# Attention and soft-MoE on one core: 128-row input tiles for later batches, a PSUM bank for each half of the first output tile, 12 one-column products, and a new instruction order

## The chip, the cores and the metric

The kernel runs on one core of one Trainium2 chip. The core has five engines with a queue each: PE (matrix products), ACT, DVE and POOL (elementwise work), and SP; 16 DMA engines carry all transfers. The metric is the device time of one launch in microseconds, the median of three runs. Before the change it is 151.72 us (151.67 to 151.9).

## The reference

Attention over four batches, eight heads, 768 positions and a head size of 64; heads with `is_retrieval` have the full causal mask, the others see four sink positions and a window of 64. Its output, 3072 rows of 512, goes through a soft mixture of eight experts with four slots each.

```python
scores = np.where(mask, scale * q @ k.T, -1e9)
a = softmax(scores); x = (a @ v)                     # [4, 8, 768, 64] -> [3072, 512]
logits = x @ phi                                     # 32 slots
slot_input = softmax(logits, axis=0).T @ x           # [32, 512]
for e in range(8):
    slot_out[e] = np.maximum(slot_input[e] @ w1[e], 0) @ w2[e]
out = softmax(logits, axis=1) @ slot_out
```

Inputs are float32: q, k and v of 6.3 MB each, and 16 expert matrices of 2 MB each (w1 and w2). The output is 6.3 MB.

## The kernel before

Every load but two small ones is issued from POOL's queue and cast to bfloat16 on its way into SBUF: 12 loads of q, k, v (one for each batch and tensor, 96 rows of 8 KB) and 16 of weights (128 rows of 8 KB), 26 MB as written. They go into 12 buffers ("slot") and, for the last four weights, into memory that attention has done with (Lw12 to Lw15).

The kernel is a list of named operations. Each declares its engine, what it depends on and which buffers it takes and gives back; the text ORDER at the head of the file is the order in which all of them are emitted, so it fixes the order on each engine. A suffix /A, /D or /P puts an operation on ACT, DVE or POOL. The names:

- Lq, Lk, Lv, Lw (line 241): loads. Tx b.c (line 389): 16 transposes on PE that bring a quarter of x of batch b into head-major form; Ex b.c (lines 234 and 236): the copy out of PSUM. V2 and VB: the same for v by key block. VF (line 456): v times a head mask.
- QK.p.g (line 408), EX.p.g (line 476), MK.p.g (line 420): scores, exponential (ACT) and mask (DVE) of head pair p (16 of them, p = 4b + n) and group g; PV.p.i (line 524) the products with v, NM (lines 535 and 537) the division, XT and XE the transposed result. QX and EXX: a last block of scores for all four pairs of a batch.
- LG, EL, TE, EG, DS, SA: logits, exponentials, dispatch sums into the slots. After the last batch: SI, SIE (the slots' inputs), H and HR (w1 and relu, line 689 and 699), TH and HE (transposes), W2.e (line 744: w2 of expert e, 16 products in four column groups, W2.7 in two halves, the first for columns 0 to 255), SO.0 and SO.1 (lines 759 and 761: each half of the slots' output, scaled), EE and RW (the combine weights and their sums).
- OMf m (line 769) and OEf m (lines 774 and 776): output tile m of 24, a product of 128 x 512 and its scaled copy out of PSUM; tile 0 is done in two halves, 0L and 0R. STf gi.r (line 804, SP's queue): the ten stores, from 256 KB to 1 MB.
- Z0 to Z67 (line 332): products of zeros, placed between the others. Z5 is eight of them between W2.6 and W2.7. "warm" is 18 of them at the start.

W2.5, W2.6 and W2.7 need the loads Lw13, Lw14 and Lw15, which are issued once the memory that they overwrite is free: Lw14 after DS.2, Lw15 after the last scores of batch 3.

Of the kernel before, what the change touches and what calls it, by code (L numbers as in the profile page):

```python
# [20 lines left out]
Lri zero warm Lq0 tables ident Lk0 keypos Tq0.3 flags Tq0.1 Z0 hm0 Eq0.1/A Tq0.2 Eq0.3/D Eq0.2/A Tq0.0 slottab  # L21
Z62 Tk0.3 Eq0.0/D Ek0.3/D ones Tk0.0 Lv0 Z60 Tk0.2 Ek0.0/D Tk0.1 Z61 Ek0.1/D Ek0.2/A QK.0.1 Tv0.1 hm3 Lw0 Lq1
Ev0.1/D EX.0.1 QK.0.0 Tv0.0 EX.0.0 QK.0.3 Ev0.0/D Lk1 EX.0.3 Tv0.2 MK.0.1 Tv0.3 Z66 hm1 Ev0.2/D QK.0.2 Ev0.3/A
Z64 MK.0.3 MK.0.0 V2.0 EX.0.2 QX.0 VB.0/A Z63 V2.3 hm2 QK.0.4 V2.1 VF.0/D VB.3/D MK.0.2 EXX.0 PV.0.0 QK.1.1
EX.0.4 V2.2 Lphi0 PV.0.1 PV.0.2 VB.2/D QK.1.0 PV.0.3 Lv1 EX.1.1 VB.1/D Lw1 Tq1.1 MK.1.1 QK.1.3 EX.1.0 MK.0.4
Tq1.0 MK.1.0 EX.1.3 QK.1.4 EX.1.4 Lw2 Eq1.0/D PV.0.4 PV.0.5 Eq1.1/D QK.2.2 Tq1.3 EX.2.2 NM.0 VF.3/P QK.1.2
VF.1/P Eq1.3/D VF.2/P EX.1.2 Tk1.3 MK.1.3 PV.1.0 QK.2.1 Tq1.2 Ek1.3/D PV.1.1 QK.2.3 MK.1.2 EX.2.1 Tk1.1 PV.1.2
MK.1.4 QK.2.0 EX.2.3 Eq1.2/D PV.1.3 PV.1.4 Ek1.1/D EX.2.0 MK.2.1 MK.2.3 Lq2 QK.2.4 MK.2.0 PV.1.5 EX.2.4 QK.3.4
Tk1.0 Tk1.2 NM.1 QK.3.3 MK.2.2 Lphi1 EX.3.4 EX.3.3 PV.2.0 PV.2.1 QK.3.0 EX.3.0 PV.2.2 Ek1.2/D PV.2.3 Lk2
Ek1.0/D XT.1 QK.3.1 MK.2.4 MK.3.3 EX.3.1 PV.2.4 PV.2.5 XE.1/D QK.3.2 XT.0 NM.2 XE.0/D EX.3.2 Tv1.1 Z67 MK.3.0  # L30
MK.3.1 QK.4.4 MK.3.2 Ev1.1/A Lv2 EX.4.4 QK.4.2 Tv1.2 Ev1.2/D MK.3.4 Tv1.0 EX.4.2 PV.3.0 PV.3.1 QK.4.0 Lw3
Tv1.3 PV.3.2 Ev1.0/D QK.4.1 Ev1.3/D PV.3.3 EX.4.0 PV.3.4 V2.4 MK.4.0 Lw4 EX.4.1 QK.4.3 VB.4/D PV.3.5 V2.6
QK.5.0 XT.2 Lw5 EX.4.3 Z65 NM.3 VB.6/A XT.3 XE.2/D EX.5.0 MK.4.1 MK.4.3 XE.3/A QK.5.3 Lq3 Tq2.1 QK.5.1 VF.4/P
MK.5.0 PV.4.0 Eq2.1/D Tq2.0 PV.4.1 EX.5.3 Tq2.2 QX.1 MK.4.2 phi PV.4.2 EX.5.1 EXX.1 PV.4.3 Eq2.2/A MK.5.1
MK.4.4 LG.0 Eq2.0/D QK.5.4 MK.5.3 Tk2.2 Ek2.2/D EL.0 V2.5 EX.5.4 PV.4.4 VB.5/D QK.5.2 TE.0 PV.4.5 Lk3 EX.5.2
MK.5.4 EG.0/D VF.5/P QK.6.0 Tk2.0 NM.4 Ek2.0/D QK.6.1 EX.6.0 MK.5.2 DS.0 QK.6.4 VF.6/P PV.5.0 EX.6.1 PV.5.1
V2.7 SA.0 PV.5.2 QK.6.2 EX.6.4 MK.6.0 PV.5.3 Tv2.1 QK.6.3 PV.5.4 PV.5.5 EX.6.2 MK.6.1 VB.7/D Ev2.1/D XT.4
QK.7.1 Lv3 EX.6.3 MK.6.4 XE.4/A Tk2.1 MK.6.2 QK.7.4 NM.5 MK.6.3 EX.7.1 Tk2.3 PV.6.0 Ek2.1/D PV.6.1 Ek2.3/D
PV.6.2 EX.7.4 QK.7.2 Tq2.3 PV.6.3 QK.7.0 Lw6 EX.7.2 MK.7.1 Eq2.3/D PV.6.4 MK.7.2 PV.6.5 EX.7.0 QK.7.3 Tv2.0
QK.8.2 EX.7.3 NM.6 Ev2.0/D EX.8.2 VF.7/P Tv2.2 Lw7 MK.7.0 QK.8.0 Tv2.3 PV.7.0 PV.7.1 QK.8.1 EX.8.0 Ev2.2/D  # L40
EX.8.1 XT.6 PV.7.2 QX.2 EXX.2 MK.7.3 Ev2.3/D V2.11 XE.6/D MK.7.4 PV.7.3 MK.8.1 VB.11/D QK.8.3 MK.8.2 V2.8
PV.7.4 QK.8.4 PV.7.5 V2.10 EX.8.3 VB.8/D MK.8.0 NM.7 EX.8.4 XT.5 QK.9.1 VF.8/P VB.10/A QK.9.3 EX.9.1 PV.8.0
PV.8.1 PV.8.2 XT.7 XE.5/D MK.8.3 MK.8.4 V2.9 QK.9.2 XE.7/D PV.8.3 PV.8.4 EX.9.3 VB.9/D QK.9.0 PV.8.5 Tq3.0
MK.9.3 VF.10/P MK.9.1 Tq3.2 EX.9.2 QK.10.2 NM.8 EX.9.0 VF.9/P Eq3.2/D LG.1 Tq3.1 EX.10.2 EL.1 Lw8 QK.9.4
Eq3.0/D MK.9.0 Tk3.2 Eq3.1/D MK.9.2 QK.10.0 PV.9.0 EX.9.4 EX.10.0 TE.1 MK.10.2 EG.1/D PV.9.1 PV.9.2 QK.10.1
Tk3.0 MK.9.4 PV.9.3 Ek3.2/D QK.10.3 Ek3.0/D EX.10.1 PV.9.4 PV.9.5 QK.10.4 EX.10.3 MK.10.0 Tk3.3 NM.9 EX.10.4
QK.11.2 Ek3.3/D DS.1 EX.11.2 PV.10.0 QK.11.0 MK.10.1 Tk3.1 PV.10.1 SA.1 EX.11.0 QK.11.1 Tq3.3 VF.11/P Ek3.1/D
# [8 lines left out]
TE.2 XT.12 QK.15.1 PV.14.0 EX.14.4 MK.14.2 PV.14.1 MK.14.3 QK.15.0 EX.15.1 PV.14.2 PV.14.3 QK.15.2 EX.15.0
MK.14.4 PV.14.4 PV.14.5 EX.15.2 XE.12/D MK.15.1 QK.15.3 EG.2/D VF.15/P XT.13 EX.15.3 QK.15.4 EX.15.4 MK.15.0
NM.14 XE.13/D DS.2 PV.15.0 XT.14 MK.15.2 MK.15.3 MK.15.4 PV.15.1 XE.14/A PV.15.2 PV.15.3 SA.2 PV.15.4 PV.15.5
NM.15 LGa.3 LTa XT.15 XE.15/D Z1 LTb ET LGb.3 Z2 Lw14 Lw15 DS.3 Z3 SA.3 SI EL.3 SIE EE.0/A Z4 H.0.1 H.0.0
HR.0.1/A H.1.1 HR.0.0/A EE.1/D TH.0 EE.2/A EE.3/D HE.0/D HR.1.1/D H.1.0 RW HR.1.0/A W2.0 W2.1 TH.1 RWR W2.2  # L60
W2.3 HE.1/D W2.4 RC W2.5 W2.6 Z5 W2.7.0 SO.0/A W2.7.1 OMf0L SO.1/D OEf0L OMf0R OMf1 OMf2 OMf3 OEf0R OMf4 OMf5
OMf6 OEf1/A OEf2/D OMf7 OMf8 STf0.0 OEf3/A OMf9 OEf7/A STf0.1 OEf8/A OEf4/D OMf10 OEf5/D OMf11 STf0.2 OMf12
OEf6/D OMf13 OEf12/A OMf14 OEf9/A OMf15 OMf16 OEf11/A STf1.0 STf1.2 OEf10/A OMf17 OMf18 OEf17/D STf2.0 OMf19
OEf13/D OEf14/D OMf20 OEf15/D OMf21 OMf22 OEf21/A OEf19/D OMf23 STf2.2 OEf16/A OEf18/D OEf22/D STf3.0 OEf23/D
STf4.0 OEf20/D STf5.0
# [76 lines left out]
def kernel(  # L142
# [40 lines left out]
    phf = sb.tile([P, 4, NS], F32, name="phf")  # L183
# [10 lines left out]
    ri = sb.tile([P, 2 * H], I32, name="ri")  # L194
# [3 lines left out]
    edist = sb.tile([P, 640], BF16, name="edist")  # L198
# [6 lines left out]

    xflat = xT.rearrange("p a c -> p (a c)")
# [51 lines left out]
    wland = [None] * NW  # L258
# [6 lines left out]
    def load_w(i, deps=()):  # L265
# [4 lines left out]
        wland[i] = load(f"Lw{i}", "POOL", 2 << 20, None if i in late_mem else wbuf[i],  # L270
                        lambda: w_view(i), src, deps=deps)
# [37 lines left out]
    def emit_slot_tables(o):  # L309
# [24 lines left out]
    tlast = [pl.op("warm", "PE", deps=[o_zero], acq=[warm], rel=[warm], emit=lambda o: emit_zero(warm, 18))]  # L334
# [16 lines left out]
    o_phi = pl.op("phi", "DVE", deps=o_ph, emit=lambda o: nc.vector.tensor_copy(  # L351
# [10 lines left out]
    for x in "qkv":  # L362
        load_qkv(x, 2)
    for i in (3, 4, 5):
        load_w(i)
    for x in "qkv":
        load_qkv(x, 3)
# [476 lines left out]
```

## Time and profile before

| | before |
|---|---|
| median of three runs | 151.72 us |
| the profiled execution | 151.93 us |
| its span, first to last instruction | 150.1 us |
| busy: PE, DVE, ACT, POOL | 131.4, 113.3, 107.7, 33.5 us |
| mean granted TensorE clock | 0.977 |
| moved by DMA | 32.91 MB |
| PE instructions: products, weight loads | 2313, 2313 |

The span is 1.8 us shorter than the execution: what lies around the program's own instructions. Busy time is an average over stages; in the page's slices each digit is a busy share in tenths. A matmul's end is modelled, so a busy PE isn't PE at its peak. "issue" in the chain is time in which the engine waited for nothing that the profile shows. Queue 0 carries the loads, queue 1 the stores, queue 8 packets of instructions.

### The profile page before, as it was taken

What the parts mean: (1) busy time and instruction counts of PE and PEld (TensorE: products, weight loads), DVE (VectorE), ACT (ScalarE), POOL (GpSimd) and SP (SyncE); (2) the same over time, 40 slices, a digit from 0 to 9 for tenths busy, and PEclk for the clock granted to TensorE, in tenths of its full rate; (3) what the DMA queues carried; (4) which work ended last, traced back from release to release, by engine and by line L of the source; (5) the groups of instructions that cost most, each with busy time, mean ns of one, the idle gap of its engine ahead of it and who ended that gap; (6) DMA issues with size and microseconds to landing.
All of it is one profiled execution on the core that took longest, in us unless ns stands there. A gap on an engine that the chain in (4) does not pass through costs nothing.

```text
span 150.1 us, 5228 instructions
## 1 busy us (share of the span) xinstructions
PE 131.4 (87%) x2313; PEld 82.6 (55%) x2313; DVE 113.3 (76%) x257; ACT 107.7 (72%) x124; POOL 33.5 (22%) x51
## 2 busy tenths in 40 slices
PE   6999799999999999999989999999899999386100
PEld 2355456677666656767856576666564376132000
DVE  3955598999879599999997999999994542187800
ACT  3023699999899999999969999999964650286100
POOL 6910004760113070502450200604120000000000
PEclk9999999999999999999999999999999999999955
DMA  3999999999999999999999999999999998059995
GB/s 36 197 216 229 214 203 215 214 224 223 200 213 215 217 218 223 218 199 219 212 215 218 227 212 216 207 223 212 223 212 212 216 216 168 11 188 410 430 419 229
DMA packets 6950, 32.91 MB, mean 219 GB/s; under 512 B 1296, under 2 KB 1296, under 8 KB 4496
## 3 DMA queue, kind: packets, MB, share of 16 engines
q0 software_dynamic: 4800, 26.22, 85.2%
q1 hardware_dynamic: 2128, 6.37, 10.8%
q8 instruction: 18, 0.29, 0.7%
q14 instruction: 4, 0.03, 0.1%
HBM read 52.50 MB, written 6.29 MB: 392 GB/s over the span
## 4 chain that ended last, share of the span: by engine, by line
PE 49%; DMA 21%; DVE 15%; ACT 3%; issue 3%; POOL 2%; DVEq 0%; POOLq 0%; ACTq 0%
PE ps L408 13%; DMA qk<-in_moe_w_dram 13%; PE ps L524 12%; PE ps L389 9%; DMA slot<-in_v_dram 8%; DVE pt L420 5%; DVE slot L776 4%; PE ps L440 3%; PE ps L549 3%; DVE xv L537 3%; ACT pt L476 2%; PE ps L332 2%; PE ps L769 2%; PE ps L563 2%; DVE qk L236 2%
## 5 line engine op out<-in xcount | busy, mean ns | idle before, releaser
L476 ACT ACTIVATE pt<-ps 128x1024 bf16<-128x1024 f32 x80 | 77.6, 1026 | 4.9 <-PE ps L408 3.5
L420 DVE TENSOR_TENSOR pt<-pt,msk 128x512 bf16<-128x512 bf16 (+1 forms) x80 | 37.8, 503 | 1.2 <-ACT pt L476 1.2
L408 PE MATMUL ps<-qk 64*128 64x512 bf16 (+3 forms) x256 | 32.5, 309 | 0.0
L524 PEld LDWEIGHTS <-pt 128*128 128x128 bf16 x640 | 24.7, 97 | 9.1 <-issue 6.4
L524 PE MATMUL ps<-vx,pt 128*128 128x65 bf16 x352 | 27.9, 193 | 0.9 <-DVE xv L537 0.7
L389 PE MATMUL ps<-ident,slot 96*64 96x96 bf16 x768 | 24.1, 208 | 1.6 <-DMA slot<-in_v_dram 0.9
L456 POOL TENSOR_TENSOR vf<-vx,fm 128x528 bf16<-128x528 bf16 x14 | 15.5, 1114 | 44.3 <-DVE vx L236 42.5
L389 PEld LDWEIGHTS <-slot 96*64 96x64 bf16 x768 | 18.9, 109 | 10.6 <-issue 7.7
L524 PE MATMUL ps<-vf,pt 128*128 128x65 bf16 x288 | 22.7, 195 | 0.0
L332 PE MATMUL ps<-zero 128*128 128x512 bf16 x66 | 19.6, 431 | 1.2 <-DVE zero L323 1.2
L236 DVE COPY qk<-ps 128x768 bf16<-128x768 bf16 x28 | 14.9, 550 | 4.6 <-PE ps L389 4.4
L537 DVE TENSOR_TENSOR xv<-ps,rs 128x768 bf16<-128x768 f32 x16 | 15.3, 958 | 0.6
L408 PEld LDWEIGHTS <-qk 64*128 64x128 bf16 x256 | 9.2, 94 | 7.2 <-issue 1.6
L241 POOL DMA_DIRECT2D slot<-in_moe_w_dram x12 | 6.8, 565 | 22.7 <-PE ps L389 16.3
L236 DVE COPY xT<-ps 128x768 bf16<-128x768 bf16 (+1 forms) x15 | 8.6, 570 | 4.2 <-PE ps L710 3.2
L332 PEld LDWEIGHTS <-zero 128*128 128x128 bf16 x66 | 6.1, 108 | 9.3 <-issue 4.8
L234 ACT COPY qk<-ps 128x768 bf16<-128x768 bf16 x4 | 3.2, 797 | 10.7 <-PE ps L389 10.7
L776 DVE TENSOR_SCALAR slot<-ps,rrow 128x512 f32<-128x512 f32 (+1 forms) x14 | 9.2, 723 | 2.2 <-PE ps L769 2.2
L236 DVE COPY xv<-ps 128x768 bf16<-128x768 bf16 x14 | 7.7, 552 | 2.0 <-PE ps L389 2.0
L769 PE MATMUL ps<-msk,xv 128*128 128x512 bf16 (+1 forms) x25 | 6.5, 369 | 2.5 <-ACT slot L774 1.3
L774 ACT ACTIVATE slot<-ps,rrow 128x512 f32<-128x512 f32 (+1 forms) x11 | 6.6, 671 | 2.1 <-PE ps L769 2.1
L549 PE MATMUL ps<-ident,xv 128*128 128x128 bf16 x96 | 8.1, 220 | 0.0
(96 smaller groups left out, 129.0 us busy)
## 6 DMA issues: line engine op xcount, KB each, us to landing
slot<-in_moe_w_dram POOLq DMA_DIRECT2D x12, 1024.0 KB, 25.4
slot<-in_q_dram POOLq DMA_DIRECT2D x4, 768.0 KB, 18.4
slot<-in_k_dram POOLq DMA_DIRECT2D x4, 768.0 KB, 21.5
slot<-in_v_dram POOLq DMA_DIRECT2D x4, 768.0 KB, 23.7
out_dram<-slot SPq DMA_DIRECT2D x3, 1024.0 KB, 6.3
out_dram<-slot SPq DMA_DIRECT2D x5, 512.0 KB, 4.3
qk<-in_moe_w_dram POOLq DMA_DIRECT2D x2, 1024.0 KB, 18.8
vx<-in_moe_w_dram POOLq DMA_DIRECT2D x1, 1024.0 KB, 21.4
```

The costliest lines, as they stand in the source:

```text
L236: nc.vector.tensor_copy(dst, src)
L332: nc.tensor.matmul(scb[buf.slot][:, 0, :], zero[:, 0:128], zero, start=True, stop=True)
L389: nc.tensor.transpose(t[64 * i:64 * (i + 1), :, s, :], rv[:, i, 8 * c + s, :], ident[0:96, 0:96])
L408: nc.tensor.matmul(scb[sc.slot][:, i, c:c + 128 * nb], kk, qq.rearrange("p b c -> p (b c)"), start=True, stop=True)
L420: e.tensor_tensor(pT[:, :, 0:w], pT[:, :, 0:w], mh[:, :, c:c + w], op=ALU.mult)
L456: e.tensor_tensor(vfs[VFb[p].slot], vv, mm, op=ALU.mult)
L476: nc.scalar.activation(pTs[PTb[b, n].slot][:, :, 512 * g:512 * (g + 1)], scb[sc.slot], ACT.Exp, scale=scale)
L524: nc.tensor.matmul(pvb[:, h, 65 * i:65 * (i + 1)], lt, rhs, start=(j == 0), stop=(j == i))
L537: nc.vector.tensor_tensor(xo, pvw[:, :, :, 0:64], r.rearrange("p i (j o) -> p i j o", o=1).to_broadcast([P, 2, 6, 64]), op=ALU.mult)
L549: nc.tensor.transpose(t[:, 128 * i:128 * (i + 1)], xv[:, i, 128 * n:128 * (n + 1)], ident)
L769: nc.tensor.matmul(bank()[:, c0:c1], out_lhs(gi, r), slot_out[:, c0:c1], start=True, stop=True)
L776: nc.vector.tensor_scalar(d, bank()[:, c0:c1], sc_, None, op0=ALU.mult)
```

## The change

Six things change together.

1. **Tiles of 128 rows.** q, k, v of batch 0 stay as they were. Those of batches 1 to 3, 9 x 96 = 864 rows, are laid end to end into seven buffers of 128 rows (the last has 96). A tensor that crosses a buffer's edge is loaded in two pieces: q3, k1, v1 and v2. A group of 16 transposes now covers 128 rows, 28 groups instead of 36, and each tensor in it has a copy of its own out of PSUM (52 copies instead of 36). QK and V2 wait only for the pieces that hold their rows (`evs`).
2. **A bank for each half of tile 0.** OMf0L and OMf0R are two units with a PSUM bank each; they shared one.
3. **One-column products.** 12 products of 128 x 1 follow the 18 of "warm".
4. **Z5 is dropped**; the eight zero products between W2.6 and W2.7 go.
5. Setup: the slot tables are split, the larger part on POOL; phi's copy goes to ACT; `edist`, `phf` and `ri` live in the memory of eT.
6. **ORDER** is a new list, with other engines for some copies: SO.0 on DVE and SO.1 on ACT, all four HR on ACT.

```diff
+    tiles = [[(x, 0, 0, 0, 96)] for x in "qkv"]
+    row = 0
+    for b_, x_ in [(b_, x_) for b_ in range(1, B) for x_ in "qkv"]:
+        r0 = 0
+        while r0 < 96:
+            if row % 128 == 0:
+                tiles.append([])
+            n_ = min(96 - r0, 128 - row % 128)
+            tiles[-1].append((x_, b_, row % 128, r0, n_))
+            row, r0 = row + n_, r0 + n_
+    tbufs = [Buf("S8") for _ in tiles]
...
+    def emit_warm(o):
+        emit_zero(warm, 18)
+        for _ in range(12):
+            nc.tensor.matmul(scb[warm.slot][:, 0, 0:1], zero[:, 0:128], zero[:, 0:1], start=True, stop=True)
...
-                        nc.tensor.transpose(t[64 * i:64 * (i + 1), :, s, :], rv[:, i, 8 * c + s, :],
-                                            ident[0:96, 0:96])
+                        nc.tensor.transpose(t[64 * i:64 * (i + 1), :, s, :], rv[:, i, 8 * c + s, :],
+                                            ident[0:rows, 0:rows])
...
+    def evs(x, b, n=None):
+
+        return [o for r0, o in ev[x, b] if n is None or r0 < 24 * n + 24]
...
-            if e == NE - 1 and not z5:
-                z5 = [fill("Z5", 8, w2o[-1:] + [o_rwm])]
...
+    if not NLEFT:
+        units[:1] = [[(0, 0, 256)], [(0, 256, 512)]]
...
-H.1.0 RW HR.1.0/A W2.0 W2.1 TH.1 RWR W2.2
-W2.3 HE.1/D W2.4 RC W2.5 W2.6 Z5 W2.7.0 SO.0/A W2.7.1 OMf0L SO.1/D OEf0L OMf0R OMf1 OMf2 OMf3 OEf0R OMf4 OMf5
+W2.0 W2.1 W2.2 W2.3
+HE.1/D W2.4 Lw15 W2.5 W2.6 W2.7.0 W2.7.1 SO.1/A SO.0/D OMf0L OMf0R OMf1 OMf2 OEf0R OMf3 OEf0L OMf4 OEf1/A OMf5
```

What the change moves on the engines shows at three places. The first is PE's queue at the end of W2.7 and the first output tiles, before: line 744 is W2.7, line 769 OMf0L, OMf0R and OMf1.

```order
L744 LDWEIGHTS xT
L744 MATMUL ps<-qk_76,xT 32x256
L769 LDWEIGHTS xv
L769 MATMUL ps<-msk,xv 128x256 [waits Activation_49]
L769 LDWEIGHTS xv [waits DVE_49]
L769 MATMUL ps<-msk,xv 128x256 [waits Activation_49]
L769 LDWEIGHTS xv
L769 MATMUL ps<-msk,xv 128x512
```

The same place after the change (line 790 is W2.7, line 815 the output tiles):

```order
L790 LDWEIGHTS xT
L790 MATMUL ps<-qk_76,xT 32x256
L815 LDWEIGHTS xv
L815 MATMUL ps<-msk,xv 128x256 [waits DVE_49]
L815 LDWEIGHTS xv
L815 MATMUL ps<-msk,xv 128x256 [waits Activation_49]
L815 LDWEIGHTS xv
L815 MATMUL ps<-msk,xv 128x512
```

Before, OMf0R waits twice: for DVE (SO.1) and for ACT, which has to read OMf0L out of the bank. After, it waits once, for SO.1, now on ACT. These rows stand at 4575 to 4582 of PE's 4628 before, and at 4327 to 4334 of 4380 after.

The second place is PE's queue at the products that wait for the last two loads. Before, between W2.6 (from xv, the load Lw14) and W2.7 (from qk, Lw15), rows 4527 to 4532:

```order
L744 LDWEIGHTS xT
L744 MATMUL ps<-xv,xT 32x256
L332 LDWEIGHTS zero
L332 MATMUL ps<-zero 128x512
L332 LDWEIGHTS zero
L332 MATMUL ps<-zero 128x512
```

After, rows 4295 to 4300:

```order
L790 LDWEIGHTS xT
L790 MATMUL ps<-xv,xT 32x256
L790 LDWEIGHTS xT
L790 MATMUL ps<-qk_76,xT 32x256 [waits DMASW7_49]
L790 LDWEIGHTS xT
L790 MATMUL ps<-qk_76,xT 32x256
```

W2.6 is now followed at once by the product that waits for Lw15. W2.5 stands in rows 4233 to 4264 and W2.6 in rows 4265 to 4296.

The third place is POOL's queue, the loads behind those of batch 0. Before:

```order
L241 DMA slot_66<-in_moe_w_dram 128x4096
L241 DMA slot_67<-in_q_dram 96x2x2048
L241 DMA slot_68<-in_k_dram 96x2x2048
L241 DMA slot_69<-in_v_dram 96x2x2048
L241 DMA slot_70<-in_moe_w_dram 128x4096
```

After:

```order
L243 DMA slot_67<-in_q_dram 96x2x2048
L243 DMA slot_67<-in_k_dram 32x2x2048
L243 DMA slot_68<-in_k_dram 64x2x2048
L243 DMA slot_68<-in_v_dram 64x2x2048
L243 DMA slot_69<-in_v_dram 32x2x2048 [waits DMASW0_49]
L243 DMA slot_70<-in_moe_w_dram 128x4096 [waits DMASW1_49]
```

k1 and v1 are two loads each and share buffers with their neighbours. A load waits for the eighth one ahead of it (DMASW), which holds before and after.

More of the change, by code (lines that the diff above doesn't have):

```diff
@@ L20 @@
 ORDER = """
[L21 to L25, printed above, removed]
@@ L31 @@
[L31 to L35, printed above, removed]
@@ L56 @@
[L56 to L60, printed above, removed]
@@ L61 @@
-W2.3 HE.1/D W2.4 RC W2.5 W2.6 Z5 W2.7.0 SO.0/A W2.7.1 OMf0L SO.1/D OEf0L OMf0R OMf1 OMf2 OMf3 OEf0R OMf4 OMf5
[L62 to L65, printed above, removed]
+zero Lri warm Lq0 tables ident keypos Tq0.3 Tq0.2 Eq0.3/A Eq0.2/A Z0 Tq0.0 flags hm0 Lk0 hm3 Tq0.1 Lv0
@@ L66 @@
+OEf20/A STf5.0
 """
@@ L374, with transposes @@
     setup = [o_fl, o_id]
-    def transposes(x, b):
-        raw = raws[x, b]
-        tb = {"q": QTb, "k": KTb, "v": VTb}[x][b]
-        dst = {"q": lambda: qTs[QTb[b].slot], "k": lambda: kTs[KTb[b].slot], "v": lambda: vT}[x]
-        ev[x, b] = []
+    def transposes(g):
+        parts, raw = tiles[g], tbufs[g]
+        rows = sum(p[4] for p in parts)
+        x0, b0 = parts[0][:2]
         for c in range(4):
@@ L421, in mask_emit @@
         return f
-    for b in range(B):
-        for x in "qkv":
-            transposes(x, b)
+    for g in range(len(tiles)):
+        transposes(g)
     tq0 = [o for o in pl.ops if o.name == "Tq0.3"]
```

263 lines of the change are left out of this document (156 added, 107 removed).

## The prediction

> **What bounds the kernel now.** I read the page's slices first, then its queues, the chain of waits from the last load on, and short stretches around that load's end.
>
> ```profile
> DMA  3999999999999999999999999999999998059995
> GB/s 36 197 216 229 214 203 215 214 224 223 200 213 215 217 218 223 218 199 219 212 215 218 227 212 216 207 223 212 223 212 212 216 216 168 11 188 410 430 419 229
> ...
> q0 software_dynamic: 4800, 26.22, 85.2%
> ...
> q8 instruction: 18, 0.29, 0.7%
> ```
>
> The DMA engines are full from the second slice to the 33rd (to about 124 us), at 200 to 229 GB/s, empty for some 5 us, and full again at 410 to 430 GB/s while the output leaves. All 26.22 MB of loads are in the first stretch, all 6.29 MB of stores in the second. PE, ACT and DVE are busy too, but what they do before the last load matters only if it makes a load or the last products late.
>
> ```profile
> 110.73 18.89 DMA qk<-in_moe_w_dram
> 129.62 0.04 issue
> 129.66 0.43 PE ps L744 x8
> ...
> 130.11 0.48 ACT msk L759
> ...
> 130.64 0.28 PE ps L769
> ...
> 130.94 0.48 ACT slot L774
> ...
> 131.47 2.01 PE ps L769 x9
> ```
>
> The chain says the same: the load of the last weights (Lw15) is seen at 129.62; then W2.7's first half, SO.0, OMf0L and OEf0L follow each other. So the end has three parts: when Lw15 lands, the steps from there to the first store, and the stores.
>
> ```profile
> xv<-in_moe_w_dram POOLq DMA_DIRECT2D x1, 1024.0 KB, 13.6
> ...
> 125.50:126.00 0.50, 0.50 (x28) 0.49 (x20) 0.00 (x0) 0.00 (x0) 0.00 (x0) 1.00 0.64 131
> ...
> 128.00:128.25 0.25, 0.18 (x1) 0.09 (x1) 0.00 (x0) 0.00 (x0) 0.00 (x0) 1.00 0.19 33
> 128.25:128.70 0.45, 0.00 (x0) 0.00 (x0) 0.00 (x0) 0.00 (x0) 0.00 (x0) 1.00 0.00 0
> 128.70:129.40 0.70, 0.00 (x0) 0.00 (x0) 0.00 (x0) 0.00 (x0) 0.00 (x0) 1.00 0.16 35
> ```
>
> Lw14 took 13.6 us from issue to landing, of which one megabyte at this rate is 4.9 us: the queue was 8 to 9 us deep even for the late loads, so no load is short of its issue. The stretches (columns: length, the five engines, clock, DMA share, GB/s) show how the loads end. The 16 DMA engines don't end together: the share falls from 0.64 before 126 to 0.19 by 128.25, and then one engine is left, which holds Lw15 until 129.4. The next rows (DMA queues, for 128.3 to 129.6 and for 125 to 126.5) show what it has left, and what put it behind.
>
> ```profile
> q8 instruction: 1, 0.02, 5.3%
> q0 software_dynamic: 2, 0.01, 3.1%
> ...
> q8 instruction: 1, 0.02, 4.1%
> ```
>
> After 128.3 two load packets remain (0.65 us of one engine), and between 125 and 126.5 there was a packet of queue 8, of 4.1% of 16 x 1.5 us = 0.98 us. Queue 8 moves 18 packets of 16 KB in the run against 4626 PE instructions: one for every 257. I read it as PE's own program, fetched block by block on the same engines. One engine that is 1.1 us behind the next is one such packet behind.
>
> **The change part by part. First term, the code packets.** PE has 4628 rows before and 4380 after (128 transposes and 8 zero products less, 12 one-column products more, each with its weight load). The queue-8 packets come by row number, so the question is where the 17th falls.
>
> ```profile
> 0.00:112.40 112.40, 108.74 (x1997) 70.97 (x1998) 97.26 (x231) 94.27 (x104) 33.53 (x51) 1.00 1.02 209
> ...
> 0.00:122.20 122.20, 118.25 (x2142) 75.74 (x2143) 102.46 (x238) 100.34 (x112) 33.53 (x51) 1.00 1.02 210
> ...
> 0.00:125.70 125.70, 121.75 (x2248) 78.82 (x2252) 103.69 (x242) 100.60 (x112) 33.53 (x51) 1.00 1.02 210
> ```
>
> Packets 16, 17 and 18 start at about 115.4, 125.2 and 128.7 (found by narrowing the stretch). Three microseconds ahead of each, PE had begun 3995, 4285 and 4500 instructions: 101, 67 and 108 rows short of 16, 17 and 18 times 256. So a packet is asked for 67 to 108 rows ahead of a block's edge and comes about 3 us later (an estimate from these rows). The edge of block 17 is row 4352. Before, that is asked for in RW and the packet hits the loads; after, rows 4244 to 4285 stand in the second half of W2.5 and in W2.6, the last two products ahead of the wait for Lw15.
>
> ```profile
> 125.27 0.61 PE L744 MATMUL ps<-vx,xT 128*32 128x256 bf16 x16
> 125.71 0.61 PE L744 MATMUL ps<-xv,xT 128*32 128x256 bf16 x16
> 126.25 1.93 PE L332 MATMUL ps<-zero 128*128 128x512 bf16 x8
> ```
>
> At the times of before, W2.5 and W2.6 start at 125.27 and 125.71, so the 17th packet would come at 128.4 to 128.8, when all engines but the late one are done, and that one is late only for its own third packet. Lw15 then lands about 1.1 us earlier. Bounds: 0 (the packet still hits the loads) and -1.1 us; I take -1.1, with the packet's time as the row it is nearest to. [...]
>
> **Second term, the banks of tile 0.** Rows of the timeline:
>
> ```profile
> 130.33 0.48 DVE L761 TENSOR_SCALAR msk<-ps,rcs 128x256 bf16<-128x256 f32 x1 [5.32 <-PE ps L744]
> 130.64 0.27 PE L769 MATMUL ps<-msk,xv 128*128 128x256 bf16 x1 [0.35 <-ACT msk L759]
> ...
> 131.78 3.16 DVE L776 TENSOR_SCALAR slot<-ps,rrow 128x256 f32<-128x256 f32 x5 [0.96 <-PE ps L769]
> 131.99 4.88 ACT L774 ACTIVATE slot<-ps,rrow 128x512 f32<-128x512 f32 x8 [0.57 <-PE ps L769]
> 132.29 10.26 SPq L804 DMA_DIRECT2D out_dram<-slot  x10
> ```
>
> SO.1 is done at 130.81 and PE is free at 130.91, yet OMf0R starts at 131.47, when OEf0L has read the bank both share. With a bank of its own it starts at 130.91: 0.56 us less. OEf0R then runs from 131.22 to 131.70 and STf0.0 goes at 131.73 instead of 132.29. OMf1 follows OMf0R, so OEf1 starts as OEf0L ends (131.43, not 131.99), and STf0.1 gains the same. Behind them ACT and DVE feed a store of 512 KB (two tiles, 1.22 us at 430 GB/s) with two evictions of 0.6 and 0.7 us on two engines, as now. The whole of -0.56 us reaches the end. SO.0 and SO.1 only swap engines (0.47 and 0.48 us).
>
> **What costs nothing here.** Shorter loops and moved work, with their rows:
>
> ```profile
> L476 ACT ACTIVATE pt<-ps 128x1024 bf16<-128x1024 f32 x80 | 77.6, 1026 | 4.9 <-PE ps L408 3.5
> ...
> L389 PE MATMUL ps<-ident,slot 96*64 96x96 bf16 x768 | 24.1, 208 | 1.6 <-DMA slot<-in_v_dram 0.9 <-DVE qk L236 0.5
> ...
> L236 DVE COPY qk<-ps 128x768 bf16<-128x768 bf16 x28 | 14.9, 550 | 4.6 <-PE ps L389 4.4
> ...
> L456 DVE TENSOR_TENSOR vf<-vx,fm 128x528 bf16<-128x528 bf16 x2 | 1.4, 701 | 0.4 <-ACT vx L234 0.4
> ...
> L236 DVE COPY elg<-ps 128x192 bf16<-128x192 bf16 x3 | 0.8, 253 | 0.2 <-PE ps L585 0.2
> ```
>
> A group of 16 transposes is 24.1/48 = 0.50 us. There are 8 groups fewer: -4.0 us of PE if a 128-row group lasts as long, +0.6 us if it lasts 128/96 as long (28 x 0.67 against 36 x 0.50). DVE has 34 copies of 768 after batch 0 now, 18.7 us; then 19 of 768, 13 of 512 and 14 of 256, at 0.55, 0.42 and 0.28 (drawn between the rows of 768 and 192): 19.8 us. With two VB and an XE more at 0.55 and two VF more at 0.70, DVE has some 4 us more; ACT has 12 copies, five of them smaller, for 13. ACT, with 80 x 1026 ns, and DVE are nearly full, so attention may end 3 us earlier or 2 us later. All of it hides behind the loads: W2.6 is done by 126.3 and Lw15 lands at 129.6, or at 128.5 after the first term, so the cover is 3.3 or 2.2 us; beyond it a microsecond costs a microsecond. Slot tables on POOL, phi on ACT, the 12 products (beside the wait for q) and QK's shorter waits have the same cover. Z5 goes too: PE then stands still from W2.6 to Lw15.
>
> **Loads cut in two.** Eight of the 12 q, k, v pieces of batches 1 to 3 are now 32 or 64 rows: 384 rows of 8 KB, 3.15 MB, 14.7 us at 214 GB/s.
>
> ```profile
> 43.00:52.00 9.00, 9.00 (x169) 6.07 (x166) 6.64 (x15) 8.58 (x12) 1.72 (x2) 1.00 1.05 213
> 54.00:67.00 13.00, 12.89 (x282) 8.90 (x280) 12.76 (x26) 12.71 (x15) 4.24 (x6) 1.00 1.02 214
> ```
>
> The first stretch loads 96-row pieces, the second 128-row weights: 213 and 214 GB/s, no loss from narrower rows. The trace has no narrower load of this size; the bounds are 0 and 14.7 us (half the rate), and I take 0, by the 96-row row.
>
> **Sum**, on the profiled execution (151.93 us, span 150.1): -1.13 - 0.56 = -1.7, 150.24. The median of the runs shown, 151.72, is 0.2 lower: **150.0 us**.
>
> **Rivals.** *The packet still hits.* If attention ends over 1.2 us earlier, W2.5 and W2.6 start before 124.4 and the 17th packet comes before 127.5, into the loads: Lw15 stays at 129.6, only the banks count, 151.15 us. For it: up to 4 us less on PE. Against it: DVE's 4 us more.
>
> *PE's clock.* In that case PE stands still for 4.5 us or more with no Z5.
>
> ```profile
> 139.90:143.30 3.40, 0.00 (x0) 0.00 (x0) 2.29 (x4) 0.00 (x0) 0.00 (x0) 1.00 1.03 426
> 143.30:149.00 5.70, 0.00 (x0) 0.00 (x0) 0.00 (x0) 0.00 (x0) 0.00 (x0) 0.50 0.91 378
> ```
>
> After its last product at 139.3, PE was granted full clock for 4 us more, then half. Before the first store stand W2.7.0 (0.43), OMf0L and OMf0R (0.28 each): between nothing and +1.0 us if they double; I take +0.45: 151.6 us. [...]
>
> *Slower: the cut loads are slow.* If pieces of 32 and 64 rows run at 85% of the rate, 14.7 us become 17.3, and Lw15 lands 2.6 us later: 152.6 us. It decides from 12% on (1.7 us). Against it: the 96-row stretch. [...]
>
> *Compute is late.* If DVE's added copies push W2.6 over 4 us later, the loads no longer end last: 152 us or more.
>
> **How the numbers follow.** Forecast 0.46, packet hits with full clock 0.23, with lost clock 0.13, cut loads slow 0.12, compute late 0.06. The range runs from 149.6 (the forecast less 0.3, as the engines before the last one end at 127.9 to 128.2, and 0.1 of spread) to 151.9 (the lost clock's 151.6 and 0.3): it leaves out the last two, 0.18. About 0.2% is what a measurement can tell from no change: faster 0.69 (the first two), same 0.15 (the lost clock and 0.02 of the slow loads), slower 0.16.
>
> **What would show it.** In the changed kernel's profile: Lw15 seen near 128.5; 16 packets of queue 8 before that and the 17th after; OMf0R directly behind OMf0L, with the first store 2.1 us after Lw15 instead of 2.7; full clock until the stores. Wrong would be: Lw15 at 129.6 with a queue-8 packet between 125 and 128; under 205 GB/s in the stretches of the cut loads; a PE wait at W2.7 for anything but the DMA.

## The result, and the profile after

| | before | after |
|---|---|---|
| median (executions) | 151.78 us (4) | 150.47 us (4, 150.38 to 150.76) |
| the profiled execution, its span | 151.93, 150.1 | 150.56, 148.8 |
| Lw15 seen by PE | 129.62 | 128.85 |
| from there to the first store's issue | 2.67 | 2.11 |

The ratio is 0.9916, with a 95% interval of 0.9899 to 0.9934: 0.8% faster, 1.3 us. Of the two terms of the sum, the banks brought what they were priced at (0.56 us) and the load's end came 0.77 us earlier where 1.13 was forecast; 1.33 together, and the spans differ by 1.3. In one experiment, the kernel called late below, a single execution of 211.84 us was disturbed and is left out.

The chain of waits of the changed kernel from the last load on (start, us, what):

```profile
111.08 17.77 DMA qk<-in_moe_w_dram
128.85 0.04 issue
128.89 0.43 PE ps L790 x8
129.31 0.03 issue
129.34 0.49 DVE msk L807
129.83 0.04 issue
129.88 0.48 PE ps L815 x2
```

The last link is new. OMf0L and OMf0R now stand in one piece; in the chain of before an ACT copy of 0.48 us stood between them. The timeline (start, us, engine, line, operation, and in brackets the idle time ahead of it and what ended it) has the rest of the end:

```profile
126.28 0.61 PE L790 MATMUL ps<-xv,xT 128*32 128x256 bf16 x16
...
128.89 0.62 PE L790 MATMUL ps<-qk,xT 128*32 128x256 bf16 x16 [2.00 <-DMA qk<-in_moe_w_dram]
...
130.96 3.03 SPq L859 DMA_DIRECT2D out_dram<-slot  x5
```

W2.6 starts 0.57 us later than before (125.71), and 2.00 us of PE's wait for Lw15 still cover it. Lw15, which waits for the last scores, was issued 0.35 us later too (111.08 for 110.73). The stretches of before, asked of the changed kernel (length, the five engines, granted clock, DMA share, GB/s):

```profile
43.00:52.00 9.00, 8.61 (x147) 5.87 (x145) 7.32 (x19) 7.56 (x11) 3.86 (x6) 1.00 1.07 215
54.00:67.00 13.00, 12.81 (x242) 8.94 (x240) 12.90 (x30) 12.34 (x14) 3.67 (x4) 1.00 1.05 219
...
128.25:128.70 0.45, 0.00 (x0) 0.00 (x0) 0.00 (x0) 0.00 (x0) 0.00 (x0) 1.00 0.16 37
128.70:129.40 0.70, 0.51 (x16) 0.34 (x15) 0.06 (x1) 0.00 (x0) 0.00 (x0) 1.00 0.00 0
```

Of the cut loads, v2 runs at the end of the first stretch and q3 between the two and early in the second; the rest of these stretches is whole loads. Asked for the cut loads alone, the changed kernel moved 219 GB/s from 24 to 31 us (k1, v1) and 216 from 48.2 to 55.6 (v2, q3), where whole ones made 213 and 214 before. After 128.70 nothing is left of the loads; before, one engine worked on to 129.4. The DMA queues between 128.3 and 129.6:

```profile
q8 instruction: 1, 0.02, 4.7%
q0 software_dynamic: 5, 0.00, 0.5%
```

The share of 4.7% of 16 x 1.3 us is one engine for 0.98 us: the 17th packet of instructions, now when queue 0 has only closing packets of 0.00 MB left (writes of 4 bytes, 512 in the trace, 16 for each of the 32 loads, the last 16 at 125.9 to 128.5; the author reads each as the end of one engine's part of a load). It starts at 128.34. The page counts 17 such packets, one less than before.

### The profile page after: what moved, and what is told of

It reads as the page before. It is cut to its first block, busy times and chain, and to the rows that moved or that the text cites. A ratio compares the mean times of both kernels' runs of the same rounds, so it can differ in the third digit from the quotient of the medians.

```text
span 148.8 us, 4992 instructions
## 1 busy us (share of the span) xinstructions
PE 127.3 (86%) x2181; PEld 81.2 (55%) x2189; DVE 112.8 (76%) x266; ACT 107.6 (72%) x128; POOL 34.8 (23%) x58
## 4 chain that ended last, share of the span: by engine, by line
PE 37%; DMA 28%; DVE 13%; ACT 6%; POOL 4%; issue 3%; DVEq 0%; POOLq 0%; ACTq 0%
DMA slot<-in_v_dram 16%; DMA qk<-in_moe_w_dram 12%; PE ps L565 10%; PE ps L450 9%; PE ps L420 7%; ACT pt L517 5%; DVE pt L462 4%; DVE xv L578 3%; POOL slot L243 3%; PE ps L815 2%; PE ps L590 2%; PE ps L604 2%; DVE slot L823 2%; PE ps L481 1%; DVE qk L238 1%
## 5 line engine op out<-in xcount | busy, mean ns | idle before, releaser
L420 PE MATMUL ps<-ident,slot 128*64 128x128 bf16 (+1 forms) x640 | 22.8, 216 | 2.1 <-DMA slot<-in_v_dram 1.0
L497 POOL TENSOR_TENSOR vf<-vx,fm 128x528 bf16<-128x528 bf16 x12 | 13.7, 1143 | 44.4 <-DVE vx L238 42.1
L420 PEld LDWEIGHTS <-slot 128*64 128x64 bf16 (+1 forms) x640 | 17.7, 109 | 10.3 <-issue 8.4
L565 PE MATMUL ps<-vf,pt 128*128 128x65 bf16 x288 | 22.8, 195 | 0.0
L238 DVE COPY qk<-ps 128x768 bf16<-128x768 bf16 (+2 forms) x35 | 15.2, 465 | 5.1 <-PE ps L420 3.9
L358 PE MATMUL ps<-zero 128*128 128x512 bf16 x51 | 15.9, 428 | 1.8 <-DVE zero L349 1.2
L238 DVE COPY xv<-ps 128x768 bf16<-128x768 bf16 (+2 forms) x21 | 8.9, 429 | 0.9 <-PE ps L420 0.7
L821 ACT ACTIVATE slot<-ps,rrow 128x512 f32<-128x512 f32 (+1 forms) x14 | 8.2, 679 | 0.5 <-PE ps L815 0.4
L236 ACT COPY qk<-ps 128x768 bf16<-128x768 bf16 (+1 forms) x5 | 3.5, 712 | 7.0 <-PE ps L420 7.0
L823 DVE TENSOR_SCALAR slot<-ps,rrow 128x512 f32<-128x512 f32 (+1 forms) x11 | 7.2, 720 | 1.7 <-PE ps L815 1.7
L238 DVE COPY vx<-ps 128x768 bf16<-128x768 bf16 x14 | 7.6, 551 | 0.6 <-PE ps L481 0.6
```

Of the source, the lines that this page charges most:

```text
L238: nc.vector.tensor_copy(dst, src)
L358: nc.tensor.matmul(scb[buf.slot][:, 0, :], zero[:, 0:128], zero, start=True, stop=True)
L420: nc.tensor.transpose(t[64 * i:64 * (i + 1), :, s, :], rv[:, i, 8 * c + s, :], ident[0:rows, 0:rows])
L497: e.tensor_tensor(vfs[VFb[p].slot], vv, mm, op=ALU.mult)
L565: nc.tensor.matmul(pvb[:, h, 65 * i:65 * (i + 1)], lt, rhs, start=(j == 0), stop=(j == i))
L823: nc.vector.tensor_scalar(d, s_, sc_, None, op0=ALU.mult)
```

## The experiments

Two theories stood against each other for each term. For the first: the 17th packet of instructions, where it falls among the last loads, holds Lw15; or the packets cost nothing and the loads ended earlier for another reason. For the second: the bank's wait reaches the end; or the stores, which keep the DMA engines full (before, 426 GB/s at a share of 1.03 from 139.9 to 143.3), take it up. All kernels compute the whole output. In the table "store" is the time from Lw15 seen to the first store's issue, both from the profiled execution, whose own time stands beside. The times of early and early2 fall in two groups, so that their medians and intervals say little.

| kernel | median us | before, same chip | ratio, 95% interval | profiled | Lw15 | store |
|---|---|---|---|---|---|---|
| changed | 150.47 | 151.78 | 0.9899 to 0.9934 | 150.56 | 128.85 | 2.11 |
| onebank | 151.06 | 151.91 | 0.9930 to 0.9957 | 151.30 | 128.71 | 2.89 |
| b_bank | 151.27 | 151.87 | 0.9932 to 0.9965 | 151.29 | 129.57 | 2.12 |
| early | 150.68 | 151.91 | 0.9896 to 0.9945 | 152.03 | 130.32 | 2.11 |
| early2 | 151.19 | 151.87 | 0.9919 to 0.9986 | 152.52 | 130.25 | 2.63 |
| early2_again | 150.36 (one) | 151.87 | | 150.36 | 128.67 | 2.11 |
| early3 | 151.42 | 151.87 | 0.9956 to 0.9987 | 151.42 | 129.68 | 2.10 |
| col0 | 150.60 | 151.91 | 0.9898 to 0.9932 | 150.88 | 129.03 | 2.21 |
| late | 151.33 | 151.91 | 0.9949 to 0.9977 | | | |
| late_again | 150.98 (one) | 151.87 | | 150.98 | 128.78 | 2.11 |
| b_cut9 | 152.06 | 151.87 | 0.9999 to 1.0024 | 152.44 | 129.75 | 2.67 |
| z5 | 150.47 | 151.87 | 0.9892 to 0.9922 | 150.63 | 128.89 | 2.11 |

### The banks: undone in the changed kernel, and made alone in the one before

onebank, against the changed kernel (the lines of ORDER are cut at both ends):

```diff
+        b1 = 0
+        if u == 0:
+            bank0 = bank
+        elif u == 1:
+            bank, b1 = bank0, 256
...
-            arg = (bank, gi, r, c0, c1, 256 * x)
+            arg = (bank, gi, r, c0, c1, 256 * x + b1)
...
-SO.0/D OMf0L OMf0R OMf1 OMf2 OEf0R OMf3 OEf0L OMf4
+SO.0/D OMf0L OEf0L OMf0R OMf1 OMf2 OEf0R OMf3 OMf4
```

> The changed kernel with tile 0's right half put back into the bank of its left half, so that OMf0R waits until OEf0L has read it. Theory (second term): the first store is issued 2.6 us after Lw15 instead of 2.07, and all of it reaches the end: +0.5 to +0.6 us, 151.0 us. Rival (the stores, which run at 430 GB/s, take up the delay): the first store is later but the end is not, 150.5 us within 0.2. Lw15 and the packets of queue 8 stay as they are.

b_bank, against the kernel before (each engine's order is kept):

```diff
+        if m == 0:
+            bank_r = banks.pop(0)[1]
...
-                      emit=lambda o, x=(bank, gi, r, c0, c1): out_mm(o, *x))
+                      emit=lambda o, x=(bank_r if nm == "R" else bank, gi, r, c0, c1): out_mm(o, *x))
```

> The kernel before with one part of the change alone: tile 0's right half gets a bank of its own. Theory (second term): Lw15 stays where it is in before (129.6), the first store goes 2.07 us after it instead of 2.63, and the time is 0.5 to 0.6 us less, 151.2 to 151.3 us. Rival (the store queue takes it up): 0, 151.8 us.

Against the kernel before on the same chip, onebank is 0.85 us faster and the changed kernel 1.31: undoing the banks costs 0.46 us. b_bank is 0.60 us faster than before, with Lw15 where it was. The second term rests on the row of OMf0R before, and on its absence in the timeline of b_bank. Before:

```profile
131.47 3.23 PE L769 MATMUL ps<-msk,xv 128*128 128x256 bf16 x14 [0.56 <-ACT slot L774]
```

b_bank:

```profile
129.61 0.62 PE L700 MATMUL ps<-qk,xT 128*32 128x256 bf16 x16 [1.41 <-DMA qk<-in_moe_w_dram]
...
130.59 3.47 PE L725 MATMUL ps<-msk,xv 128*128 128x256 bf16 x15 [0.35 <-ACT msk L715]
...
131.69 2.29 SPq L762 DMA_DIRECT2D out_dram<-slot  x4
```

OMf0R no longer waits for the copy that reads OMf0L out of the bank (0.56 us before; the 0.35 us here are OMf0L's wait for SO.0), and the store goes at 131.69. The stores hide nothing here: all ten stand in SP's queue, behind the first. In onebank the same wait is back, but the store is 2.89 us after Lw15 instead of 2.67; the rest has another cause, shown below with the clock.

### The 17th packet: rows added ahead of it

Three kernels move the packet by adding PE rows early, as products of one column, and one is run again. early has 73 more near the start, in place of Z0 and four of the Z6x:

```diff
-        return pl.op(name, "PE", deps=deps, acq=[z], rel=[z], emit=lambda o: emit_zero(z, n))
+        k = {"Z0": 45, "Z61": 12, "Z62": 12, "Z63": 12, "Z64": 12}.get(name, 0)
+        return pl.op(name, "PE", deps=deps, acq=[z], rel=[z],
+                     emit=lambda o: emit_ones_col(z, k) if k else emit_zero(z, n))
```

> The changed kernel with 73 one-column products more near its start (146 PE rows with their weight loads), so that block 17 of PE's program ends 146 rows earlier in the work. Theory (code packets): the 17th packet of queue 8 is then asked for in W2.0 to W2.2, comes between 126 and 128 instead of at 128.34, and holds one of the eight late DMA engines, which now end their loads between 128.2 and 128.5, for 0.95 to 1.1 us more: Lw15 is seen at 129.6 to 129.95 instead of 128.85, and the time is 0.8 to 1.1 us more than the changed kernel's (151.3 to 151.6 us). Rival (code fetches are hidden; Lw15 came earlier in the change for another reason, such as the tiles of the loads): Lw15 stays at 128.85 and the time at 150.5 us, within 0.2.

Missed, and told why by its trace. Ten of 12 executions lie between 150.37 and 150.84 us, two at 152.03 and 152.57; the profile is of the 152.03. The work came later (mean granted clock 0.930 instead of 0.965), so the packet hardly moved against the loads: Lw15's own issue came at 112.11 instead of 111.08. But in the execution of 152.03 us Lw15 was seen only at 130.32. So the next kernel, early2, puts the rows where they cost no time, in place of the tail's Z1 to Z4; early3 does both.

```diff
-        k = {"Z0": 45, "Z61": 12, "Z62": 12, "Z63": 12, "Z64": 12}.get(name, 0)
+        k = {"Z1": 28, "Z2": 10, "Z3": 28, "Z4": 10}.get(name, 0)
```

> The changed kernel with its eight zero products of 512 columns in the tail (Z1 to Z4) replaced by 76 of one column, which take as long (24 of them 0.75 us, one of 512 0.27 us) but make 136 PE rows more, all ahead of W2.0: unlike the run with 146 rows near the start, whose work came 1 us later, the work keeps its time and block 17's edge comes 2 us earlier in it. Theory (code packets): the 17th packet is served between 125.8 and 127.6, among the last loads of one of the late engines, and Lw15 is seen at 129.4 to 130.3 instead of 128.85: 0.6 to 1.5 us more than the changed kernel's 150.5, in nearly all executions (in the run before this one only 2 of 12). Rival (that run's slow executions had another cause; packets cost nothing): Lw15 at 128.85, 150.5 us within 0.2.

Half of it came: six executions at 150.34 to 150.59 us, six at 151.79 to 152.71, none between. The profile is of 152.52. The DMA queues of early2 from 128.6 to 129.6, and the chain's load:

```profile
q0 software_dynamic: 1, 0.00, 0.1%
```

```profile
111.07 19.18 DMA qk<-in_moe_w_dram
130.25 0.04 issue
```

One packet of queue 0, of 0.00 MB, is left behind the packet of instructions: the closing write of one engine's part of Lw15. In the changed kernel this stretch holds no packet at all. All data had landed by then, yet PE saw Lw15 only at 130.25, 1.4 us later than in the changed kernel. Only half of that lies ahead of the closing write, which stands at 129.2 (the last one of the changed kernel at 128.5). From 129.25 to 130.3 no packet moves on any queue, and PE sees Lw15 some 1.0 us behind the closing write, where it took 0.3 us in the changed kernel. What fills these 0.7 us, no row shows. The place within the last load that the expectation named (125.8 to 127.6) was wrong: the packet starts at the very end of that engine's loads, and two orders are possible there. An execution of the other group shows the second one:

> The same kernel as the run with 136 rows more in the tail, whose times fell in two groups (150.34 to 150.59 and 151.79 to 152.71); its profile was of the second, with the 17th packet between the last data and the closing 4-byte packet of one engine. Theory: in an execution of 150.3 to 150.6 us the 17th packet starts after that engine's closing packet, and Lw15 is seen at 128.6 to 128.9; in one of 151.8 or more it is ahead of it again, and Lw15 is seen at 130.2. Rival: the packet's place is the same in both.

It took 150.36 us. Its stretch from 128.6 to 129.6 has no packet of queue 0, as in the changed kernel; the packet of instructions lies between 128.2 and 129.4 as before. The chain's load, and the timeline:

```profile
111.17 17.50 DMA qk<-in_moe_w_dram
128.67 0.04 issue
```

```profile
128.71 0.62 PE L796 MATMUL ps<-qk,xT 128*32 128x256 bf16 x16 [0.31 <-DMA qk<-in_moe_w_dram]
```

Lw15 is seen at 128.67 with the same program. PE was 1.3 us later here (its pause is 0.31 us instead of 3.19), yet the packet starts at 128.21, no later than in the other execution (128.24); it came behind the closing write of its engine, not ahead of it. Whether PE's lateness decided that order, one execution of each kind doesn't show.

> The changed kernel with both earlier additions: 146 PE rows near the start and 136 in the tail, 282 in all. The first delay the work by 1 us (62 rows), so block 17's edge comes some 220 rows, 3.5 us, earlier in the work, against 68 and 136 rows in the two runs before, where the 17th packet landed right at the end of one engine's loads (128.24 to 128.32) and hit in 2 and 6 of 12 executions. Theory (code packets): now it is served well inside the last load, 125.5 to 127.3, as in the kernel before (125.2), in every execution; one engine ends its loads at 129.3 to 129.5, Lw15 is seen at 129.6 to 129.8 and the time is 0.8 to 1.1 us above the changed kernel's 150.5, with no executions near 150.5. An 18th packet follows where the 17th stood and does little. Rival (the slow executions of the two runs before come from something else): times in two groups again, or 150.5 us.

As expected: seven executions between 151.30 and 151.65 us and none near 150.5, 0.95 us above the changed kernel. The queues of early3 from 126.3 to 127.6, and its chain:

```profile
q0 software_dynamic: 18, 0.14, 52.0%
q8 instruction: 1, 0.02, 4.7%
```

```profile
112.66 17.02 DMA qk<-in_moe_w_dram
129.68 0.04 issue
```

The packet (0.98 us of one engine) stands among the data of the last load, and Lw15 is seen 0.83 us later than in the changed kernel. This is the state of before, made again in the changed kernel by nothing but rows of PE. That early3 also issued Lw15 1.58 us later isn't the cause: of Lw15's 16 closing writes, 15 stand no later than in the changed kernel (up to 128.4), and one alone at 129.4, as one did before (129.3). What was not expected is in its timeline:

```profile
127.45 0.50 PE L797 MATMUL ps<-vx,xT 128*32 128x256 bf16 x11
128.84 0.38 PE L797 MATMUL ps<-vx,xT 128*32 128x256 bf16 x5 [0.90 <-issue]
...
129.72 0.62 PE L797 MATMUL ps<-qk,xT 128*32 128x256 bf16 x16
```

PE stopped for 0.90 us in the middle of W2.5's 16 products, with no semaphore to wait for. It went on more than 1.2 us after that packet's end, which lies ahead of 127.6. That it waited for its program is the author's guess: the profile names no releaser. The wait for Lw15 just hid it: W2.7 follows at 129.72.

### The 12 one-column products, and fewer rows

col0 leaves out the 12 one-column products (the last two lines), late also cuts Z0 from 8 to 2 and each Z6x from 3 to 1; late_again is the same kernel as late.

```diff
-        return pl.op(name, "PE", deps=deps, acq=[z], rel=[z], emit=lambda o: emit_zero(z, n))
+        k = {"Z0": 2, "Z6": 1}.get(name[:2], n)
+        return pl.op(name, "PE", deps=deps, acq=[z], rel=[z], emit=lambda o: emit_zero(z, k))
...
-        for _ in range(12):
+        for _ in range(0):
```

> The changed kernel without its 12 one-column products (24 PE rows fewer, 4356): block 17 ends 24 rows later in the work. Theory: the 17th packet is asked for in W2.6 or in its wait, comes at 128.5 to 129 or later, behind the last loads still: Lw15 at 128.85, the time within 0.2 us of 150.5. So the 12 products are not what brought the gain; what did is the 256 rows of transposes and zero products that went. Rival (the 12 products matter): the packet meets the first products or stores, or the cover beside the wait for q is needed, and the time is 0.3 to 1.0 us more.

150.60 us, 1.31 below before, as the changed kernel is: the 12 products make no difference that shows here. By the count of rows, the part of the change that moved the packet is then the 256 rows of transposes that went; Z5's rows stood behind it.

> The changed kernel without the 12 one-column products, and with its early zero products cut from 8 to 2 (Z0) and from 3 to 1 (the eight Z6x): 4312 PE rows, so block 17 does not exist. Theory: 16 packets of queue 8 remain, the 17th (128.34 in the changed kernel) is gone, and since it stood behind that engine's last load, nothing changes: Lw15 at 128.8 to 128.9, time within 0.2 us of 150.5. Rival (the packet at 128.34 still delayed an engine or the first products): Lw15 or the first store 0.3 to 1.0 us earlier, time 149.5 to 150.2. Second rival (the zero products near the start keep PE's clock): PE's first products run slower, attention ends later; hidden up to some 2 us, the time unchanged by that.

Wrong: 0.58 us faster than before where 1.3 was expected; eleven executions lie between 150.94 and 151.97.

> The same kernel as the run without the 12 one-column products and with the shortened zero products (4312 PE rows), for a profile that is not disturbed: its times were 0.8 us above the changed kernel's, its profile that of an execution in which every product took twice as long. Theory to be tested: with fewer zero products near the start PE comes to full speed later (products of the first 20 us take twice as long for longer), attention ends later than the cover of 2 us, and W2.6 ends after Lw15's landing or Lw14 and Lw15 are issued late. Rival: attention ends as before and the 0.8 us is lost after Lw15 (slower last products for want of a warm clock) or in the landing of Lw15.

Neither. There are still 17 packets, so the count of blocks in late's expectation was off. The queues of late_again between 130.9 and 132.1:

```profile
q1 hardware_dynamic: 65, 0.13, 28.7%
q8 instruction: 1, 0.02, 5.7%
```

The 17th packet, with 5.7% of 16 x 1.2 us = 1.1 us, now stands where the first store (queue 1) begins. Lw15 (128.78) and the first store (2.11 us later) are as in the changed kernel, and the span is 0.4 us longer (149.2). So the time was lost among the stores. The clock was also halved there (0.50 from 130.17 to 133.58). b_cut9, with the PE rows of before (whose last packet starts at 128.73, 3.6 us ahead of the first store), lost as much behind its first store (0.4 us) with its clock halved (0.50 from 132.04 to 135.45), which speaks for the clock in this execution; what makes late's median 0.86 us longer than the changed kernel's stays open. The gap between the last load and the first store showed no cost of a packet.

### The cut loads, on the kernel before

```diff
-        lands[x, b] = [load(f"L{x}{b}", "POOL", 96 * 2 * 8192, buf, lambda: raw_view(buf), raw_src(x, b))]
+        cut = ((0, 32), (32, 96)) if b else ((0, 96),)
+        lands[x, b] = [load(f"L{x}{b}" + (f".{r0}" if b else ""), "POOL", (r1 - r0) * 2 * 8192, buf,
+                            lambda r0=r0, r1=r1: raw_view(buf)[r0:r1], raw_src(x, b)[r0:r1]) for r0, r1 in cut]
```

> The kernel before with all nine q, k, v loads of batches 1 to 3 (7.08 MB) issued in two pieces of 32 and 64 rows, nothing else changed. In the changed kernel four loads are cut and its engines are 0.18 us later at the end of the loads. Theory (a small fixed cost for each piece more, 0.04 us): Lw15 0.3 to 0.5 us later, the time 0.3 to 0.5 us more, 152.1 to 152.3 us. Rival (pieces of 32 and 64 rows run at a lower rate): at 85% some 5 us more. Null: 0, and the 0.18 us have another cause. [...]

Lw15 comes 0.13 us later and the median is 0.19 us higher, with an interval that touches no change: even the small fixed cost was put too high, and the lower rate is excluded. The stretches of b_cut9:

```profile
43.00:52.00 9.00, 9.00 (x168) 6.03 (x164) 7.67 (x15) 8.48 (x10) 4.30 (x7) 1.00 1.07 214
54.00:67.00 13.00, 12.81 (x276) 8.59 (x275) 12.08 (x26) 12.67 (x15) 4.33 (x6) 1.00 1.03 216
```

The first stretch carries cut pieces, at 214 GB/s; the second has the whole weights, as before (216 GB/s for 214). The larger pieces of the first lie in rows 32 to 95 of their buffers. Pieces of 64 rows in rows 0 to 63 and 64 to 127, with 32 rows each beside them, are in the changed kernel (v2 and q3), which moved 216 GB/s there.

### Z5 back, and what the pause does to the clock

The line of ORDER is cut behind W2.7.1.

```diff
-HE.1/D W2.4 Lw15 W2.5 W2.6 W2.7.0 W2.7.1
+HE.1/D W2.4 Lw15 W2.5 W2.6 Z5 W2.7.0 W2.7.1
...
+        if e == NE - 1 and not z5:
+            z5 = [fill("Z5", 8, w2o[-1:] + [o_rwm])]
```

> The changed kernel with Z5 back (eight zero products of 512 columns between W2.6 and W2.7, which occupy PE for 1.9 of the 2.0 us that it waits for Lw15). Theory: the clock of the last products was kept without them, so nothing is gained; they end before Lw15 lands: time within 0.2 us of 150.5. Rival (PE's pause costs the last products or the first evictions speed): 0.2 to 1.0 us less. Second rival (Z5 ends after Lw15 has landed, as PE is 0.6 us later than in before): up to 0.3 us more.

150.47 us, the changed kernel's median; their intervals overlap for the most part. But the theory's reason, that the clock is kept without Z5, holds only for some executions. Stretches of PE's busy time in the execution of the changed kernel that was profiled, then in onebank and in col0; each is 3.41 us long, as the half-clock stretch of early2_again is (118.28 to 121.69, last rows of this text), and laid so that the changes of the granted clock fall on the edges of such stretches:

```profile
124.80:128.21 3.41, 2.09 (x80) 1.00 0.65 135
128.21:131.62 3.41, 2.31 (x24) 1.00 0.02 5
```

```profile
125.69:129.10 3.41, 1.56 (x54) 1.00 0.38 79
129.10:132.51 3.41, 2.40 (x17) 0.50 0.01 4
```

```profile
126.83:130.25 3.42, 0.81 (x17) 1.00 0.21 46
130.25:133.66 3.41, 3.19 (x9) 0.50 0.48 168
```

The work is the same in all three up to W2.7, with a pause for Lw15 of 2.00, 1.85 and 2.29 us. In the changed kernel it falls across an edge: PE is busy for 61 and 68% of the two stretches, and both ran at full clock. In onebank and col0 it falls into one stretch, busy for 46 and 24%, and the next 3.41 us ran at half clock (6.8 in onebank: 0.50 from 131 to 133, 0.63 on average from 133 to 137). In onebank the first products were slower (W2.7 0.76 us for 0.62, OMf0L 0.37 for 0.27), which is why its store went 0.2 us later than the bank alone explains. Of col0's six executions the two with a mean clock of at most 0.960 took 150.88 and 151.03 us, the other four 150.39 to 150.72; of the changed kernel's four, the one at 0.957 took 150.76, the others at most 150.56; of onebank's six, the one at 0.955 took 151.30, the others 150.94 to 151.21. The four with Z5 took 150.41 to 150.63. By the means of these groups, of one or two executions each, the pause costs some 0.25 to 0.45 us in some executions (an estimate: where the clock was halved is shown for the profiled ones alone); Z5 changes nothing in the median.

## Why the prediction was right, and where it was off

**The bound** (loads to the end, then the tail, then stores) was read rightly: each kernel's time followed Lw15 and the first store. From there to the end of the span it took 17.8 to 17.9 us in every profile but those of late_again (18.3) and b_cut9 (18.2).

**First term, the code packets.** Sign and cause hold: early3 brings before's state back by rows alone, and one kernel, early2, has both outcomes. The size is what missed, -0.77 for -1.13. The working took the late engine's lag behind the next one (closing writes at 129.34 and 128.21) as the gain, not the packet's 0.98 us. In the changed kernel the last engines close at up to 128.51, 0.30 us later, and PE sees Lw15 0.06 us later behind that (0.34 us for 0.28); these 0.36 us are the miss. Nine cut loads cost 0.13, so the rest is not settled (over the six profiles with the packet behind the data, Lw15 moves by as much, 128.67 to 129.03). Across the profiles, Lw15 is seen at 129.57 to 129.75 where the packet stands among the data (before, b_bank, b_cut9, early3; mean 129.66) and at 128.67 to 129.03 where it stands behind (six profiles; mean 128.82). The difference, 0.83 us, is the term; the forecast's 128.5, read from one engine's neighbour in one execution, lies below all six. The rule that a packet is asked for 67 to 108 rows ahead of a block's edge and comes 3 us later was near for the changed kernel (128.4 to 128.8 forecast, 128.34 measured) but is not a clock: 136 rows more in early2 left the packet's place almost unchanged (128.24). That the late engine was late for "its own third packet" was the author's estimate: the profile names no engine. And there was luck in it. The eight engines that end last close from 128.22 on, so the packet, if it went to one of them, came at most 0.12 us behind its engine's closing write; in early and early2, at 128.32 and 128.24, it went either way. None of the 14 executions of the changed kernel, col0 and z5 shows the bad order (at most 151.03 us).

**Second term, the banks.** Mechanism and size hold: -0.56 forecast; 2.67 to 2.11 in the profile, -0.60 alone on the kernel before, +0.46 when undone.

**What costs nothing.** Right: W2.6 starts 0.57 us later, within the bounds of 3 us earlier to 2 later, and 2.00 us of cover remain. PE's transposes took 22.8 us for 24.1, between the two bounds (the upper one, 28 x 0.67 less 36 x 0.50, is 0.8, not 0.6).

**Loads cut in two.** 0 taken; b_cut9 gives 0.13 us for nine cuts at Lw15, so four cuts are below what can be seen. The cut tensors make 13 pieces, not 12, eight of them short. The rival of slow cut loads is excluded by the changed kernel's own 219 and 216 GB/s: no run shows its 85% of the rate, nor the half rate of the bound.

**PE's clock.** The rival tied it to a pause of 4.5 us, after an early end of attention. That pause did not come, but a shorter one was followed by half clock in some executions (1.85 us in onebank, 2.29 in col0), so the "full clock until the stores" holds only for others, as for the changed kernel's profile (2.00 us). The price taken for it, 0.45 us, is the upper end of what they show (0.25 to 0.45).

**Compute late, packet still hits:** neither happened.

## What to carry to other kernels

Where the last load is bound by DMA, look which engine ends last and what its last foreign packet was; here a packet of instructions cost one of them a microsecond (0.98 us). Its place moved with the count of PE instructions ahead of it, among the data of the last load with 282 rows more (early3) and to the start of the first store with 68 fewer (late_again), but hardly with 136 more (early2, 128.24 for 128.34). In early3 that count alone moved the time by 0.95 us. Ahead of the first of ten stores that move 410 to 430 GB/s, the wait of 0.56 us counted nearly in full (0.46 and 0.60). What a pause of PE does to the granted clock should be read from stretches of the trace (3.41 us here), over several executions, not from its length in one.

## What the runs showed of the hardware

- **A packet of instructions ahead of a closing write cost more than one among the data.** Among the data it held Lw15 0.83 us; between one engine's last data and its closing write of 0.00 MB it was 1.4 us (130.32 and 130.25 for 128.85), of which 0.7 passed behind the closing write, where no packet moved; their cause is open. This was seen in the profiled executions of early and early2, of which 2 and 6 of 12 took over 151.7 us.
- **Half of the engines closed the last load later.** In the changed kernel eight of Lw15's 16 closing writes stand at 125.9 to 127.0 us and eight at 128.2 to 128.5. Sixteen packets of instructions in turn on the eight late engines would be 1.9 us for each of them, and the 17th the first that gives one a third: an estimate from the 0.94 us that a packet took on average and from this count of eight. The profile doesn't name the engines.
- **Half clock followed the stretches of 3.41 us in which the pause for Lw15 left PE least busy.** PE was busy for 24, 26, 36, 41 and 46% of the stretch (col0, early2, late_again, b_cut9, onebank), and the next ran at half clock; at 50, 57, 61 and 82% (b_bank, before, changed, z5) the next ran at full clock. None of the five was idle throughout. The change to half clock came at 129.10 us in onebank, 129.64 in early2, 130.17 in late_again, 130.25 in col0 and 132.04 in b_cut9. These are nine executions, and the share alone doesn't decide it: in onebank the stretch from 129.10 to 132.51 was busy for 70%, and the next ran at half clock too. In early2, at half clock from 129.64, the first store went 2.63 us after Lw15 for 2.11, 0.52 us more.
- **Half clock also followed a stretch with most of the one-column products.** In early2_again the stretch with most of the 76 shows PE busy for 3.27 of 3.42 us, and the next one was granted half clock (rows below). The executions of early and early3, which have such products near the start in place of some of 512 columns, have a mean clock of 0.918 to 0.946, those of the changed kernel 0.957 to 0.966. Whether the one-column products are the cause was not shown.

```profile
114.86:118.28 3.42, 3.27 (x81) 1.00 0.98 206
118.28:121.69 3.41, 3.41 (x54) 0.50 1.07 223
```
